# Attention and gated FFN on one core: the second to sixth pairs' queries reach the other row half by SBUF-to-SBUF transfers, with a new order of the work

## The chip, the cores and the metric

The kernel runs on one core of a Trainium2 chip. The metric is the device time of one execution in microseconds (us), the median of three runs. A profiled execution comes beside them, and all rows below are from it.

## What is computed

Queries, keys and values come as 4 batches of 8 heads, 1152 rows of 64 numbers, in float32. Neighbouring query rows are averaged, so 576 queries stand against 1152 keys. The attention's result goes through a feed-forward block with a gate.

```python
q_pool = q.reshape(B, H, S // 2, 2, D).mean(axis=3)
scores = (1 / np.sqrt(D)) * np.matmul(q_pool, k.transpose(0, 1, 3, 2))
attn = softmax(scores)                       # rowwise, with the maximum taken off
x = np.matmul(attn, v)                       # then heads side by side: (4, 576, 512)
h = np.maximum(x @ w_in, 0.0)                # (4, 576, 1024)
conv = sum(conv_w[t] * shifted(h, t) for t in range(3))
out = (h * sigmoid(conv)) @ w_out            # (4, 576, 512)
```

## The kernel before, in words

Two heads make a pair (16 pairs, four to a batch). The head with e = 0 has its queries in partitions 0 to 63 of a tile, the one with e = 1 in 64 to 127. `loads` brings in a pair: the keys to a `kt` tile, the values, and the queries to `qin`, of which there is a single buffer for all pairs. It then adds the two query rows that are to be averaged (`sum_q`, L305, on POOL or DVE), and makes two tiles from the sum: `qt` (`keep_q`, L308, ScalarE, all 128 partitions and 640 columns) and `qd` (`turn_q`, L313 on DVE or L318 on ScalarE, 64 partitions and 512 columns each, twice), which holds the same numbers with the two heads' row halves exchanged. A head's scores against half of its keys come from `qt`, and against the other half from `qd`, since those keys lie in the other row half of `kt`. So all of a pair's scores but those of its last 64 queries need both tiles.

`softmax` takes a pair through five steps of 128 queries (the fifth has 64). In each step and head: the scores (PE, L466), their maximum (DVE, L479), the exponential with its sum (ACT, L484), a small sum and its inverse (ACT L497 or DVE L501, then DVE L507). Most heads then write the normalised probabilities as two float16 parts (`hl`: the high one on ACT L532 or POOL L527, the low one on DVE L535) and have them turned by a DMA transpose (SP, L549). Eight heads (the set `X32`, one or two in each of the first four pairs, one in the fifth, the sixth and the tenth) normalise in float32 (L572 on POOL or DVE, L568 on ACT), are turned by PE (L586), and copied out of PSUM into `pt` by ACT (L595) or DVE (L597). `values` multiplies by the values (PE, L618 and L624) and splits the result (L640, L646, L651). `feed` and `second` are the feed-forward block (PE L713, L934, L940, L928). The weights' tidying up at the start runs through ACT L1017 and L1069, DVE L1030 to L1046, POOL L1021 and DVE or POOL L1050.

Nothing here is ordered by the compiler. All work is written down as tasks, and three tables set the rest: `ORDER` is the order in which the tasks are issued, each on the queue of its engine; `SLOTS` says which buffer of a ring a tile gets; `SWAPPED` names the tasks that run on their second engine (ACT instead of POOL, DVE instead of ACT, and so on). Each engine, and SP with its DMA issues, works through its own queue strictly in order. All loads, stores and transposes are issued by SP, on one DMA queue.

Of the kernel before, what the change touches and what calls it, by code (L numbers as in the profile page):

```python
# [94 lines left out]
cIcGaacMcOcNcPcHhtcJcKasabachucYhwadcQaecRhvafcThxcShPaghycUahhzhScXhAcWhBcVhQaic5cLathIaBhEhThRc4auhLhMavhFaw  # L95
hJhNhKaxibhUayazhOhVaAhWh4hCicajbEhGcZc8hDdriehHeoiddohXh5ifc7hsaCdah6c9aDaEh7aFhYh8aGhZh9akaHc0ixigiaalaIh0c1
ihamaJh2iiiyijiAh1aKbFh3andcimiziqikiBinaoiliodbirapiCdpiTc6isaqipiDivaLiEiUitiFiwjgiuaMiViMiKjhiGiLiHiIaNariR
aOiWjjiSaTc2iXaPjii3iJiPjkiNiYjyiOiQjlaQi6jzi4aRi7ddiZjBjmdsaUdwi0jnaVi5i1jCaSjvi8jAa2jwi2deaWjDaXdudtaYjQjoi9
jEdvdfjFaZjtjGdhdJjTa0dijxjudja3jRjpbGjrjqa4c3jUjsjJjNjSjcdka5a1dljOdmbbdnjVdMjKa6dOjWjLjddLjXa7j8j5jPjYjMbcjH
j9dgjZjIbdkbj0a8kabedqj3a9kcj1j4kqdNbfkddPkDj6d5bakedxbgj7kfkrknkgbhkskokLj2bwktdybiklkMkEkOkmd8kpkudzkNkjkPkh  # L100
bjkyk3kQbkkkkvkBk4bxkik6kRkCkSkwk0blkzkTbmkAkxbnk5dBdCk7fnkWewbybokYkXbsdDkUdEk1llk8dFk2lmdGealokVk9ebdHkHbqla
lplbdKlibpd9ljlqbHkZlkbrlnlclDbIkIlrldlsbJlAltlelEd7lgdIlGlhdQlBlFludRbKlVlHlfbLdSlwlvlWlIbubUlyd4epdTlxlXlCmg
btlJlzlKlYlLlSdVmhmjbVdWbWlOmklMlPlNlQdXlTl8mibzbXmlbAlZdYbBbYdZbZmmlUd0mnmvb0dAmyd2mol0mwlRl9mpb1mBmzmqmamtbM
mCmAmrl3mud1mQmDl1d6msl6mEl7l4mFmRl2mNmGmTl5mSjamxmLmUesmJmKbNmHjbmOm8mVbOmMm9nbmIkFedmPbPetmckGbQeud3bRmWbSmX
ncbTm5nabCdUm6b2mYnqndm7mbevm3mdbvm4m1nem2nDnfnrnnb3eJngerb4ecb5eenob6nsnhefb7nLb8nEnteLninjnMnFmZnknOm0menunv
nGbDb9ehDznyeinNcinPnpnlkJDAejnwn3nQDBnBeknmeln6eNDCemnRnCnSn4nTnWnzC7nAnxcjn7DUckC8n5clnUDlDVC9cmnZDmDan0nXn8
# [1142 lines left out]
```

## Time and profile before

| | |
|---|---|
| median of three runs | 605.52 us (605.26 to 607.05) |
| the profiled execution | 606.64 us |
| its span, first to last instruction | 604.8 us |
| mean granted clock of TensorE | 0.997 of 2.4 GHz |
| PE busy | 576.2 us (95%) |
| DVE busy | 563.0 us (93%) |
| ACT busy | 446.3 us (74%) |
| POOL busy | 282.6 us (47%) |
| DMA queue q1, share of 16 engines' span | 84.7% |

The profiled execution lasted 606.64 us; 1.84 us of it lie outside the span, and it is 1.12 us above the median. Busy time says how long an engine had at least one instruction running. An engine's shares are means over stretches of different kinds: before the first keys have landed nothing can run, then the weights and the first pairs share the engines, then attention and feed-forward alternate, and at the end only the feed-forward block is left.

### The profile page before, as it was taken

The numbers are of one execution on the slowest core, as the hardware profiler recorded it, in microseconds if no ns is written. First come the engines' busy times: TensorE is split into PE (matmuls) and PEld (weight loads), VectorE is DVE, ScalarE is ACT, GpSimd is POOL, SyncE is SP. The second block draws the span as 40 slices with busy tenths as digits, with TensorE's granted clock in tenths as the row PEclk, the third lists the DMA queues.
The fourth block names the chain that finished last, engine by engine and source line by source line (L and its number), as shares of the span: only waits on it lengthen the run. The fifth ranks groups of instructions, "written<-read, shape, count | busy, mean of one in ns | idle before, by whom it ended". The sixth has DMA issues, their size and how long they took to land.

```text
span 604.8 us, 11969 instructions
## 1 busy us (share of the span) xinstructions
PE 576.2 (95%) x4454; PEld 349.7 (58%) x4454; DVE 563.0 (93%) x911; ACT 446.3 (74%) x854; POOL 282.6 (47%) x300
## 2 busy tenths in 40 slices
PE   5989988799999999999999999999999999999997
PEld 2545555366665665556565665565657456775753
DVE  4999999899999999999999999999999999999881
ACT  4999999889999988767786956567567766776431
POOL 1563644626454533463545655645532435434530
PEclk9999999899999999999999999999999999999999
DMA  4944959684949899999999699899897999997601
GB/s 152 351 151 128 178 111 256 130 191 94 214 86 276 167 184 224 192 220 209 193 196 212 151 209 224 150 216 222 212 204 168 191 175 166 171 177 140 103 18 62
DMA packets 266713, 106.97 MB, mean 177 GB/s; under 512 B 254368, under 2 KB 255648, under 8 KB 266656
## 3 DMA queue, kind: packets, MB, share of 16 engines
q1 hardware_dynamic: 266656, 106.21, 84.7%
q8 instruction: 35, 0.57, 0.4%
q14 instruction: 22, 0.18, 0.1%
HBM read 37.77 MB, written 4.72 MB: 70 GB/s over the span
## 4 chain that ended last, share of the span: by engine, by line
PE 38%; DVE 15%; issue 4%; ACT 4%; POOL 3%; DMA 2%; SPq 0%; POOLq 0%; DVEq 0%; ACTq 0%
PE s L466 9%; PE a L934 8%; PE a L618 7%; PE a L713 7%; DVE hl L535 6%; DVE sm L479 4%; PE a L928 3%; DVE g L742 3%; POOL hl L527 2%; DMA pt<-hl 2%; PE a L940 2%; ACT p L484 1%; PE a L624 1%; DVE g L752 1%; PE a L586 1%
## 5 line engine op out<-in xcount | busy, mean ns | idle before, releaser
L484 ACT ACTIVATE p<-s,sm 128x1152 f32<-128x1152 f32 x144 | 175.3, 1218 | 57.2 <-DVE sm L479 24.2
L479 DVE TENSOR_REDUCE sm<-s 128x1 f32<-128x1152 f32 x144 | 193.1, 1346 | 10.8 <-PE s L466 10.4
L466 PE MATMUL s<-kt,qt 64*128 64x128 f32 (+2 forms) x704 | 183.1, 473 | 8.5 <-DMA kt<-in_k_dram 5.0
L535 DVE SCALAR_TENSOR_TENSOR hl<-p,sm,hl 128x1152 f16<-128x1152 f32 (+1 forms) x111 | 160.6, 1453 | 2.2 <-POOL hl L527 1.5
L527 POOL TENSOR_SCALAR hl<-p,sm 128x1152 f16<-128x1152 f32 (+1 forms) x65 | 85.7, 1322 | 129.0 <-DVE sm L507 82.0
L466 PE MATMUL s<-kt,qd 64*128 64x512 f32 x256 | 144.6, 647 | 1.0 <-DMA kt<-in_k_dram 1.0
L618 PE MATMUL a<-pt,v 128*64 128x256 f16 (+2 forms) x1512 | 111.9, 271 | 1.8 <-DMA pt<-hl 1.8
L466 PEld LDWEIGHTS s<-kt,qt 64*128 64x128 f32 (+1 forms) x704 | 77.3, 175 | 51.3 <-ACT p L484 20.9
L713 PE MATMUL a<-x,wi 128*128 128x257 f16 (+3 forms) x864 | 103.8, 274 | 1.5 <-ACT h L724 0.7
L713 PEld LDWEIGHTS <-wi 128*128 128x128 f16 x864 | 77.2, 98 | 37.5 <-issue 18.3
L618 PEld LDWEIGHTS <-v 128*64 128x64 f16 x1512 | 86.7, 110 | 20.3 <-issue 15.5
L735 POOL TENSOR_SCALAR g<-h,cw 128x255 f32<-128x255 f32 (+3 forms) x69 | 51.6, 751 | 61.5 <-ACT h L724 53.9
L934 PE MATMUL a<-wo,g 128*128 128x512 f32 x160 | 75.7, 606 | 0.5 <-ACT h L724 0.5
L742 DVE SCALAR_TENSOR_TENSOR g<-h,cw,g 128x255 f32<-128x255 f32 (+3 forms) x144 | 70.9, 512 | 4.3 <-POOL g L735 3.9
L586 PEld LDWEIGHTS a<-ident,p 128*128 128x128 f32 (+1 forms) x360 | 37.3, 142 | 56.3 <-ACT pt L595 16.2
L532 ACT ACTIVATE hl<-p,sm 128x1152 f16<-128x1152 f32 (+1 forms) x46 | 57.6, 1252 | 15.8 <-DVE sm L507 8.1
L572 POOL TENSOR_SCALAR p<-p,sm 128x1152 f32<-128x1152 f32 (+1 forms) x32 | 43.6, 1363 | 49.5 <-DVE sm L507 39.0
L586 PE MATMUL a<-ident,p 128*128 128x128 f32 (+1 forms) x360 | 55.4, 277 | 10.9 <-ACT pt L595 7.0
L624 PE MATMUL a<-pt,v 128*64 128x256 f32 (+1 forms) x288 | 64.1, 409 | 0.0
L724 ACT ACTIVATE h<-a,bs 128x257 f32<-128x257 f32 (+3 forms) x64 | 30.7, 482 | 28.1 <-PE a L713 16.6
L934 PEld LDWEIGHTS a<-wo,g 128*128 128x128 f32 x160 | 28.1, 190 | 37.3 <-issue 32.5
L595 ACT ACTIVATE pt<-a 128x384 f32<-128x384 f32 (+2 forms) x93 | 42.5, 474 | 6.4 <-PE a L586 6.2
(140 smaller groups left out, 655.6 us busy)
## 6 DMA issues: line engine op xcount, KB each, us to landing
qin<-in_q_dram SPq DMA_DIRECT2D x15, 640.0 KB, 4.7
kt<-in_k_dram SPq DMA_DIRECT2D x15, 576.0 KB, 5.5
vin<-in_v_dram SPq DMA_DIRECT2D x9, 576.0 KB, 4.9
g<-in_moe_w_in_dram SPq DMA_DIRECT2D x8, 512.0 KB, 5.3
w<-in_moe_w_out_dram SPq DMA_DIRECT2D x8, 512.0 KB, 4.7
out_dram<-o SPq DMA_DIRECT2D x16, 256.0 KB, 3.1
pt<-hl SPq DMA_TRANSPOSE x120, 5.0
v<-in_v_dram SPq DMA_DIRECT2D x6, 288.0 KB, 4.2
```

What stands on the lines that cost most here:

```text
L466: nc.tensor.matmul(out=w, lhsT=f, rhs=kk, start=True, stop=True)
L479: nc.vector.tensor_reduce(out=sm[:, e:e + 1], in_=runs(st[e]), axis=AX.XY, op=ALU.max, negate=True)
L484: nc.scalar.activation(out=p.tile().rearrange("p (a n) -> p a n", a=2), in_=runs(st[e]), func=AF.Exp, bias=sm[:, e:e + 1], scale=1.0, accu ...
L527: eng.tensor_scalar(out=hl[rows, 0], in0=ps_[e][rows], scalar1=sm[rows, 6 + e:7 + e], scalar2=1.0, op0=ALU.mult, op1=ALU.mult,)
L532: nc.scalar.activation(out=hl[rows, 0], in_=ps_[e][rows], func=AF.Copy, scale=sm[rows, 6 + e:7 + e])
L535: nc.vector.scalar_tensor_tensor(out=hl[rows, 1], in0=ps_[e][rows], scalar=sm[rows, 6 + e:7 + e], in1=hl[rows, 0], op0=ALU.mult, op1=ALU.s ...
L586: nc.tensor.transpose(w[:, (i - a1) * nq:(i - a1 + 1) * nq], ps_[e][rows, i * P:(i + 1) * P], ident[rows, rows])
L618: nc.tensor.matmul(out=to, lhsT=o.v[:, e, c, vc:vc + D], rhs=o.pt[y, e][:, hl * NC + c, 0:n], start=(c == 0 and j == 0), stop=(c == NC - 1 ...
L624: nc.tensor.matmul(out=to, lhsT=o.v[:, e, c].bitcast(F32), rhs=p32.rearrange("p (a n) -> p a n", a=NC)[:, c, 0:n], start=(c == 0), stop=(c ...
L713: nc.tensor.matmul(out=w[:, 0:n], lhsT=wi[:, a, j, f * P:(f + 1) * P], rhs=x.x[:, c, s0:s0 + n], start=(i == 0 and j == 0), stop=(i == 2 a ...
L742: nc.vector.scalar_tensor_tensor(out=c, in0=h[:, t:t + tok], scalar=cw[:, f, t:t + 1], in1=c, op0=ALU.mult, op1=ALU.add)
L934: nc.tensor.matmul(out=w.tile(), lhsT=g[f // 4][:, f % 4, c:c + P], rhs=wo[:, f, :], start=(f == 0), stop=(f == FC - 1),)
```

## The change

For the pairs 1 to 5 (the second to the sixth) `turn_q` is gone. Instead SP issues two transfers from `qt` to `qd`, one for each head, of 64 partitions by 512 float32 (128 KB), after `keep_q` has written `qt`. The pair's scores wait for `keep_q` and both transfers. Pair 0 and the pairs 6 to 15 do as before. The three tables are new as well: the order on every queue, the buffers, and which tasks run on their second engine.

```diff
             tq = add("ACT", act(n, 0.03), lambda cols=cols: keep_q(cols), after=[t], uses=[o.qin] + ([o.qt] if i else []),
                      takes=[] if i else [o.qt])
-            ready = [tq] + [
+            if 1 <= o.pr <= 5:
+                def swap_q(e):
+                    nc.sync.dma_start(out=o.qd.tile()[D - D * e:P - D * e, :], in_=o.qt.tile()[D * e:D * e + D, 0:K1])
+
+                ready = [tq] + [
+                    add("SP", 0.3, lambda e=e: swap_q(e), after=[tq], uses=[o.qt] + ([o.qd] if e else []),
+                        takes=[] if e else [o.qd], dma=0.9) for e in range(2)
+                ]
+            else:
+              ready = [tq] + [
                 add("ACT", act(turned.stop - turned.start, 0.16), lambda eng, e=e, turned=turned: turn_q(eng, e, turned), after=[t],
                     uses=[o.qin] + ([o.qd] if e or i else []), takes=[] if e or i else [o.qd],
                     alt=("DVE", 0.08 + (turned.stop - turned.start) / 1900.0, True)) for e in range(2)
...
 ORDER = """
-cIcGaacMcOcNcPcHhtcJcKasabachucYhwadcQaecRhvafcThxcShPaghycUahhzhScXhAcWhBcVhQaic5cLathIaBhEhThRc4auhLhMavhFaw
+eccIewcYcGaacMcJcOcNcPcHhtcKasabcLbEcQacc7adhuhwaehvcUafcRcThxcScVhPatcWaghyahhzaihShAhQhBcZaBcXhIhRc5hChTauhE
...
```

The counts of instructions that the order prints, before and now: on ACT `qd<-qin 64x512` 25 and 20, `qd<-qin 64x256` 1 and 0, `hl<-p,sm 128x1152` 41 and 39, `v<-vin,vs 128x18x64` 3 and 1, `v<-vin,vs 128x9x64` 2 and 4, `x<-xf,bs` 2 and 5. On DVE `qd<-qin 64x512` 5 and 0, `qd<-qin 64x256` 1 and 2, `p<-p,sm 128x1152` 2 and 1, `xf<-a,vs 128x320` 2 and 0. On POOL `hl<-p,sm 128x1152` 64 and 66. On PE the counts are the same. On SP `qd<-qt 64x512` 0 and 10.

Lines behind L327 stand nine lines further down in the changed kernel: L549 is L558 there, L595 is L604, L484 is L493, L1017 is L1026, L1069 is L1078 and L1013 is L1022.

The first place is SP's queue around the second pair (pair 1). Before, with the pair's queries loaded first and no transfer:

```order
8 L267 DMA qin<-in_q_dram 128x1280
9 L272 DMA v<-in_v_dram 128x1152
10 L1013 DMA g<-in_moe_w_in_dram 128x1024
11 L264 DMA kt<-in_k_dram 128x1152
12 L1013 DMA g<-in_moe_w_in_dram 128x1024
13 L1013 DMA w<-in_moe_w_out_dram 128x1024
14 L272 DMA v<-in_v_dram 128x576
15 L264 DMA kt<-in_k_dram 128x1152 x2
```

and now, with the two transfers (L329) and a load of weights between them:

```order
11 L1022 DMA g<-in_moe_w_in_dram 128x1024
12 L267 DMA qin<-in_q_dram 128x1280
13 L1022 DMA g<-in_moe_w_in_dram 128x1024
14 L264 DMA kt<-in_k_dram 128x1152
15 L272 DMA vin<-in_v_dram 128x576
16 L329 DMA qd<-qt 64x512
17 L1022 DMA g<-in_moe_w_in_dram 128x1024
18 L329 DMA qd<-qt 64x512
19 L264 DMA kt<-in_k_dram 128x1152 x2
```

The keys of later pairs (the row with x2) stand behind both transfers now, and the second transfer stands behind a load that has to wait for a free buffer of `g`.

The second place is ACT's queue at the same pair. Before, with the copy to `qd` (L318) ahead of the one to `qt` (L308):

```order
18 L595 ACTIVATE pt<-a 128x3x128
19 L1069 ACTIVATE g,ws<-wo 128x512
20 L351 ACTIVATE x,vs<-v 128x2x576
21 L484 ACTIVATE p,sm<-s,sm 128x1152
22 L1017 ACTIVATE g<-g 128x512
23 L318 ACTIVATE qd<-qin 64x512
24 L308 ACTIVATE qt<-qin 128x640
25 L595 ACTIVATE pt<-a 128x3x128 x2
```

and now:

```order
20 L1078 ACTIVATE g,ws<-wo 128x512
21 L1026 ACTIVATE g<-g 128x512
22 L604 ACTIVATE pt<-a 128x3x128 x3
23 L493 ACTIVATE p,sm<-s,sm 128x1152 x2
24 L604 ACTIVATE pt<-a 128x3x128
25 L308 ACTIVATE qt<-qin 128x640
26 L604 ACTIVATE pt<-a 128x3x128
27 L1078 ACTIVATE g,ws<-wo 128x512
```

The copy to `qd` is gone, and the copy to `qt` comes one exponential and four copies to `pt` later than it did.

## Rows read from the trace of the kernel before

**Rows 1.** Busy time by stretch; columns: window, length, PE, PEld, DVE, ACT, POOL, clock, DMA, GB/s.
```profile
0.00:15.12 15.12, 8.36 (x23) 3.97 (x24) 7.54 (x14) 7.16 (x15) 2.93 (x11) 1.00 0.48 152
15.12:136.08 120.96, 108.95 (x754) 62.20 (x751) 115.15 (x191) 109.91 (x215) 59.73 (x61) 0.99 0.75 187
136.08:211.68 75.60, 73.62 (x562) 47.84 (x561) 73.99 (x126) 70.28 (x131) 40.31 (x40) 1.00 0.76 167
211.68:408.24 196.56, 195.84 (x1450) 119.09 (x1447) 191.40 (x279) 141.82 (x258) 98.44 (x97) 1.00 1.02 199
408.24:559.44 151.20, 147.97 (x1251) 91.18 (x1248) 147.04 (x232) 102.96 (x195) 65.54 (x68) 1.00 0.97 183
```

**Rows 2.** Waits of the whole core, 15.12 to 136.08 us: total us, times, longest.
```profile
PEld a L586 <- ACT pt L595: 11.7, 17, 1.0
PE a L586 <- ACT pt L595: 7.0, 12, 1.7
PEld s L466 <- ACT p L484: 5.4, 8, 1.2
PE s L466 <- ACT p L484: 2.1, 5, 0.7
```

**Rows 3.** Groups by line and form, 15.12 to 136.08 us: count, busy us, mean ns.
```profile
L318 ACT ACTIVATE qd<-qin 64x512 f32<-64x512 f32 x6 | 3.8, 629 | 0.1
L313 DVE TENSOR_SCALAR qd<-qin 64x512 f32<-64x512 f32 x4 | 1.7, 422 | 0.1
```

**Rows 4.** Groups by line and form, whole span.
```profile
L532 ACT ACTIVATE hl<-p,sm 128x1152 f16<-128x1152 f32 x41 | 51.4, 1252 | 15.8 <-DVE sm L507 8.1 <-issue 2.3 <-DVE vs L369 1.3
L568 ACT ACTIVATE p<-p,sm 128x1152 f32<-128x1152 f32 x6 | 7.5, 1252 | 0.3 <-DVE sm L507 0.2
L405 ACT ACTIVATE v<-vin,vs 128x576 f16<-128x576 f32 x2 | 1.6, 780 | 0.0
L644 ACT ACTIVATE x<-xf,bs 128x256 f16<-128x256 f32 x2 | 1.0, 516 | 0.0
L731 ACT ACTIVATE g<-h,cw 128x255 f32<-128x255 f32 x2 | 1.0, 515 | 0.0
L484 ACT ACTIVATE p<-s,sm 128x1152 f32<-128x1152 f32 x144 | 175.3, 1218 | 57.2 <-DVE sm L479 24.2 <-DVE hl L535 17.6 <-POOL hl L527 3.2
L595 ACT ACTIVATE pt<-a 128x384 f32<-128x384 f32 x79 | 37.2, 487 | 5.8 <-PE a L586 5.6
```

**Rows 5.** Timelines of ACT, DVE, PE and SP at pair 1: start, length us.
```profile
25.15 0.75 ACT L308 ACTIVATE qt<-qin 128x640 f32<-128x640 f32 x1
33.01 0.42 DVE L313 TENSOR_SCALAR qd<-qin 64x512 f32<-64x512 f32 x1
35.62 0.37 PE L466 MATMUL s<-kt,qt 64*128 64x128 f32 x1
27.83 0.33 SPq L1013 DMA_DIRECT2D g<-in_moe_w_in_dram  x1
```

**Rows 6.** DMA issues: count, KB each, median us to landing.
```profile
g<-in_moe_w_in_dram SPq DMA_DIRECT2D x8, 512.0 KB, 5.3
out_dram<-o SPq DMA_DIRECT2D x8, 64.0 KB, 2.1
out_dram<-o SPq DMA_DIRECT2D x16, 256.0 KB, 3.1
qin<-in_q_dram SPq DMA_DIRECT2D x1, 384.0 KB, 6.1
```

**Rows 7.** Busy time in stretches around a gap of PE; columns as in rows 1.
```profile
107.50:109.00 1.50, 0.00 (x0) 0.00 (x0) 1.50 (x2) 1.45 (x3) 1.50 (x2) 1.00 1.35 280
109.00:112.00 3.00, 2.89 (x9) 1.23 (x9) 1.11 (x1) 2.27 (x4) 2.62 (x3) 0.57 0.41 142
112.00:113.20 1.20, 1.20 (x7) 1.02 (x6) 1.05 (x1) 0.22 (x1) 0.00 (x0) 0.64 0.00 0
```

**Rows 8.** Chain that ended last, in order of time: start, length us.
```profile
422.04 7.24 DMA pt<-hl
```

More of the change, by code (lines that the diff above doesn't have):

```diff
@@ new lines @@
+j5jYjpj9drkbjPjqdgj6bcjZkabdkcbGj0kqjda9kdj7bej3krj1j4kLbabfkeksbgkDbwbhdPj2ktkfkMknkgdxbikukodybjklkvkOkmbxkp
+kEbkkNkykhkPkjkiblkwkQk3kkbmkxkRdzkzkSk4k0kTkBk6kCdAk1k5kWbyk7kAd8kXkUdBllbnk8dCbsdDdEkYdFkVlmlok9bqdGkZladHd9
+kHlibolpdKk2lbljlnbplqeabrlgdRlDbHlhbIlrlGkIlsdSlEltlklclebJldlAlHlFlulBlfeplVlvd7bKlIbLlylWlwbUbzlJlKmgbteblX
+lClLlzmhmjlYlxbulSdTlMmklOlNlPdVdWlQbVlTl8mibWmlbAdXdYbBbXlZdZbYl0l3lUmmmyl9bCbZd2mBmnb0mvmomzd0b1mtd3lRmCmumr
+mpmsdUbMl1mql4mDl6mwl2mAmQd1mEl7d6mFmamGmxl5mTmRmNmSkFmHmUbDbNmLm8mOmMmJbOmImVmPm9esmcedbPeekGbQmWd4mXbRm5mbbS
@@ new lines @@
+mKm6nanbbTkJjanqncmdmYb2eternDeJndbvm7jeefnenfnrngnnjbegnonjb3nLnknEb4mekKnsnhb5m3b6nintb7nFfgmZnum4b8m0m1nGnv
+ehb9nMnOm2nyeicinNnlejekDzelnPeLnmemC7DAnwnQnBn3enC8nxnRDBn6cjnSn4nTnCeueNnzeqeMDlDCnpnWnAn5n7DUckDmC9nUnZDVn0
+nXDWnVn8cln1cmooDncnolnYDoexcon9nHcpoaomoeobeOopn2eZongvcaoceyDaodoqDXojDYoDDpDZDborokDDnIosohoEotnJofowoGDcog
+evoiouoFoxDse1oyoHovcbozDqoVDEDdccezoADtoIDreBDecdeCD0DuceoJDGDfoKDvoOoWDgoBDHoCDwoPoXcfoTnKpgcgoQDhpjoUcheDoY
+phoLoRDIcqDxoZo8pko0fzo3DioSDypieEoMDjDFploNjfo4mfpyo1e2pBo9pmo5eFpnpzpopro2o6DNo7ppcreYD1DOe3DPpCpqeGpsD2cspt
@@ new lines @@
+DJpupAD8ctDkcupvDQpDpweHpQcveKpEpxpTeIpFcwD9e4pRcxpcpGfhDRD3pUpSEapHpJDSD4pIpVDKD5pMD6pWEbqqDLpdpXpNp1eQpKqrcy
+pOpYp8pPpLqsDTfjp4p9p2p5p3p6DMqtquqbp7pZqveRqyEtqcp0qaeSqdqwqzqLqAD7qeqOczqfqMqgEuqBEfeTqjqCqPqNqhqoEgqZEheUqQ
+qiqpEvqmq0qkcAqneAq2qlcBq1qREwqSExqDqxqWq3EyqTqXEcq4qUrdflq5EirgqVEzq6eVrareeWEmqErhq7EHqYEnrfrbEOq8rirrEjq9rj
+EPrkcCfkrurlrsEkqHrorvrtrcEofmElrmrprwEprFrqrxEIryeXrCEVrzqIrGEJrWrHrDrnrOEdEQrXERrYfxrIcDe0rJESrErKrArZsaEqcE
+ErEWrPrLr0EAfAsbr1cFEXrNscEee5ePEsr2soEKrBEBE1r3ELfCfEsdr4spETfBEYr7e6serMECr5E9EZr8sqe7FaEDsfr9e8EEsre9fDfasg
@@ L154 @@
+    "11210013011100101001123120001032000103030021100001131102003000100011001101133011312112101200002020011210011130"
+    "0021311100201031010310120011001001"
 )
 SWAPPED = """
[L156 to L158 removed]
@@ L159 @@
[L159 to L161 removed]
+ahalaqauaDaIaMaVa4a9bdbibqbsbybGbObWb4ccckcscAcMcOcPcUcWcXc8dmdsdGd0emgShzhHhVh1isiuiDiLiOjejmjojujvjEjGjKjNke
+kmkvkFk9lblilrlAlSlYmmmEmImNmWnengnnnAnEnJnRnToboeogoroAoJoYpapepmpEpJpLpNpYqeqgqpqtqFqJqWq7rjrlrorxrzrQrUr4r7
@@ L162 @@
+slswsIsNsTsVs1s5tdtftrtttKtVtYucuguouquGuIu0u9vgvlvnvvvHvLvTvVvYv7v9wcwlwqwzwEwMwSwWw4w9xixnxwxBxKxMxPxXx3x7yf
+yhykytyvyyyHyMyVyXy0y6y8zezizmzuzzzIzNzWzYz1AaAcAfAlAtAxAAABAOAXAZA2BbBdBpBrBABIBMBQBYCcCeChCqCvCECPCRCXC1C5DB
+DIDPDWD3EaEhEoEvECEJEQFtFAFHFOFVF2F9GgGmGnGuGBGIGPGWG3HaHNHUH1H8IeIfImIsItIAIHIOIVI2I9JgJnJuJDJFJPKwKDKKKRKYK5
+LcLjLsLuLyLFLMLTL0L7MeMlMuMwMzMAMHMNMOMVM2M9NfNgNmNn
 """
```

101 lines of the change are left out of this document (39 added, 62 removed).

## The prediction
> **What bounds the kernel now.** I read the busy times by stretch first, since the means over the whole span hide where time is left. TensorE is idle for 604.8 - 576.2 = 28.6 us in all. By stretch that is 6.8 us up to 15.1 (the first loads), 12.0 us from 15.1 to 136.1, 2.0 us up to 211.7, 0.7 us up to 408.2, 3.2 us up to 559.4, and the 3.9 us that remain at the end [rows 1]. PE's own work does not change in count, so a gain has to come out of these waits. The pairs 1 to 5 are prepared within the stretch with the 12.0 us. There DVE is busy for 95% (115.2 of 121.0), ACT for 91% (109.9) and PE for 90% (109.0): three engines that hand each step of the softmax round, none of them with much room. Behind it, from 211.7 to 408.2, PE is busy for 99.6%, and what is won ahead of that stretch passes through it.
>
> Next the waits in that stretch. The largest ones of PE and of its weight loads are for ACT: for the copies of turned probabilities (L595) 7.0 us on PE, and for the exponential that frees a score buffer (L484) 2.1 us [rows 2]. The waits of weight loads overlap PE's work, so only the PE rows are lost time. PE is thus held up by ACT more than by DVE, though DVE is the fuller engine, and it feeds ACT with the maxima.
>
> **The change part by part.** *Removed.* In the stretch six copies on ACT at 629 ns and four on DVE at 422 ns belong to the pairs 1 to 5: 3.8 us of ACT and 1.7 us of DVE [rows 3].
>
> *Moved.* With the tables also other work changes engine. I compared the two orders up to the same point, the first step of pair 6: on DVE the rows ahead of the 55th maximum, on ACT those ahead of the 55th exponential. By then DVE has five copies less (one more belongs to pair 6 and went to ACT): 5 x 0.422 = 2.1 us; its other differences run from -1.1 to +0.7 us a kind and sum to -0.1. So DVE is relieved by 2.2 us. On ACT five copies less give 3.1 us, four high parts (L532, 1.252) less 5.0 us, and one normalisation (L568) less 1.3 us. Against that stand two value splits (L405, 0.780) more, 1.6 us, five of L644 (0.516) more, 2.6 us, two of L731 (0.515) more, 1.0 us, and small ones, 0.4 us. So ACT is relieved by 3.1 + 5.0 + 1.3 - 1.6 - 2.6 - 1.0 - 0.4 = 3.8 us [rows 3, 4]. POOL takes the high parts; it is busy for half of the stretch [rows 1], so this is free, unless a high part is late there: then the low part on DVE waits.
>
> *What the relief is worth.* The lower end is nothing, if each step still waits for the engine that was not relieved at that step. The upper end is both in a row, 2.2 + 3.8 = 6.0 us, half of PE's idle time there. I take the middle between DVE's and ACT's, 3.0 us: PE waits for ACT, but ACT's maxima come from DVE.
>
> *Added: ten issues and ten transfers of 128 KB.* An issue takes SP 0.33 us [rows 5], 3.3 us for all. No row of PE in this stretch names a DMA [rows 2], and the DMA share there is 0.75 [rows 1], so I cost issues and traffic at nothing. With that cover gone, 1.3 MB at the 187 GB/s of the stretch would be 7 us of queue time.
>
> *Added: a wait on SP.* The transfers wait for `keep_q`, and all later issues wait behind them: at pair 1 two loads of keys, one of values, and the queries of pair 2. Those keys and queries are needed a pair or more later, so this is nothing too. In return `qin` is free after one copy instead of three, so later queries load earlier. That is no gain either, as no row of PE waits for queries here [rows 2].
>
> *Added: a longer way to the scores.* `keep_q`, issue and landing now come one after the other. At the pairs 2 to 5 the order leaves many softmax steps in between. At pair 1 it is tight. Before, `keep_q` ended at 25.9 and the last copy at 33.4, and the scores began at 35.62 [rows 5]. In the new order ACT has, ahead of `keep_q`, one exponential more (1.2 us and 0.2 for its sum), four copies to `pt` more (4 x 0.487) and a small sum more (0.2), and two copies to `qd` less (0.6 and 0.4): 2.3 us later, 28.2 [rows 4]. Between the two transfers stands a load of weights, which has to wait for a buffer that ACT gives back after a copy to `pt` and a sum over weights, 1.3 us later: 29.5. The second transfer is then issued near 29.9. Nearest in size are stores of 64 and 256 KB, which land after 2.1 and 3.1 us: 32.0 to 33.0, ahead of the scores. If it only lands with the load ahead of it, 5.3 us after 29.5, it is 34.8 to 35; by the slowest rows, 6.1 and 7.24 us after the issue, it is 36.0 to 37.1, up to 1.5 us late [rows 6, 8]. I take 0.4 us, nearer to the stores and the load, with the ends 0 and 1.5.
>
> The Trainium skill (DMA: Bandwidth & Descriptors, section Anatomy of one DMA) states, for transfers issued by GpSimd, about 2.0 us for any transfer and its bytes at 436 GB/s on top. By it, as an estimate, 128 KB would land after 2.3 us, this term would be 0 and the time 602.5. No run here shows it for a transfer within SBUF.
>
> *At the start* the first sum went from POOL to DVE and the first two exchanged copies stand on DVE. The second half of the first keys is issued one load later in return. I cost both at nothing.
>
> **The sum.** -3.0 + 0.4 = -2.6 us. The profiled execution took 606.64 us, so one like it would take 604.0. It is 1.12 us above the median of 605.52, and against the median the forecast is 602.9 us. With both bounds of the relief and the wait it runs from 599.5 (all 6.0) to 607.0 (no relief, 1.5 of waiting). A measurement of this kernel can tell about 0.3% from no change, which is 1.8 us: faster means below 603.7, slower above 607.3.
>
> **The rivals.** *Forecast, 602.9, chance 0.50*, of which 0.43 lie below 603.7. For it speak that both engines that hold up PE are relieved in the stretch where PE waits, and that PE is the bound behind it.
>
> *DVE decides, 604.8, chance 0.20.* DVE is the fullest engine from 15 to 136 and busy for 97% up to 559 [rows 1]. If its order sets the pace there too, ACT's relief is worth nothing, and of DVE's 2.2 us about half comes through, since a maximum taken earlier then waits for its scores: 1.1 - 0.4 = 0.7, which gives 604.8. Against it speaks PE's 99.6% from 211 to 408.
>
> *The second transfer of pair 1 is late and the clock falls, 608.9, chance 0.17; this is the way to a slower kernel.* Before, PE stood still for the whole stretch from 107.5 to 109.0, and from 109.0 to 113.2 the granted clock was 0.57 and 0.64, most of the way to the lower level of 1.2 GHz. That cost 3.0 x 0.43 + 1.2 x 0.36 = 1.7 us beyond the standstill [rows 7]. If the transfer lands 1.7 us or more after PE has come to the scores, which is the length of the longest wait there [rows 2], the same happens again: 1.7 + 1.7 = 3.4 us. PE is then the late engine, ACT and DVE run into full buffers, and their relief is worth nothing: 605.5 + 3.4 = 608.9. It decides from a landing at 37.3, 7.4 us after the issue; the slowest landing in the rows is 7.24 us [rows 8]. The load of 512 KB right ahead of it speaks for it.
>
> The Trainium skill (DMA: Bandwidth & Descriptors, section Queues, rings and completion order) says that a queue's descriptors are taken in ring order on each DMA engine. By that the transfer would come behind the weights in any case, which is this rival's condition. The trace's single queue q1 agrees, but no row shows a small transfer behind a large one.
>
> *The new order decides elsewhere, 599.7, chance 0.13.* The tables are new to the end. In the stretch from 408 to 559 PE idles for 3.2 us [rows 1]. If these go as well, it is 602.9 - 3.2 = 599.7; if they double, 606.1. This is also the case in which the transfers don't do what they are put in for: gain or loss would then be in a stretch without any. I give 0.10 to the first and 0.03 to the second.
>
> **How the numbers follow.** Faster: 0.43 + 0.10 = 0.53. The same: 0.07 + 0.20 + 0.03 = 0.30. Slower: 0.17. The range from 599.5 to 609.0 takes in the bounds of both terms and the time of the slower rival; beyond its ends remain about 0.08 on each side. The forecast's own range is 599.5 to 604.5.
>
> **What would show it.** Right: PE's idle time from 15 to 136 us is about 9 us instead of 12.0, the waits for L595 (now L604) and L484 (now L493) are shorter, the first scores of pair 6 come some 3 us earlier, and PE is full from 210 to 400. The ten transfers land in 2 to 5 us, and PE waits for none but perhaps the second one of pair 1. Wrong: a row in which PE waits for `qd<-qt` for over 1.5 us with a lower granted clock behind it; DVE without a gap and PE with as much idle time as before; or an unchanged first 210 us and a difference after 400.

## The result, and the profile after

The changed kernel took **609.41 us** (median of 4 runs, 608.85 to 610.29) beside 605.75 us for the kernel before (4 runs, 605.26 to 607.05). The ratio is 1.0064, with an interval from 1.0044 to 1.0084: slower by 3.9 us, where 2.6 us less was forecast. The profiled execution took 609.48 us with a span of 607.7; against the 604.8 of before, that is 2.9 us more.

The first view is the busy time by stretch of the changed kernel, in the columns and stretches of [rows 1].

```profile
0.00:15.12 15.12, 7.50 (x20) 3.31 (x22) 7.44 (x14) 7.07 (x15) 1.28 (x10) 1.00 0.71 245
15.12:136.08 120.96, 109.10 (x757) 64.52 (x757) 114.72 (x190) 105.40 (x210) 69.52 (x61) 0.97 0.75 185
136.08:211.68 75.60, 73.26 (x570) 48.42 (x569) 74.36 (x122) 70.17 (x135) 39.13 (x37) 1.00 0.74 169
211.68:408.24 196.56, 192.38 (x1401) 114.79 (x1396) 190.50 (x280) 142.08 (x250) 97.45 (x93) 1.00 1.00 194
408.24:559.44 151.20, 149.55 (x1217) 92.94 (x1218) 146.86 (x226) 102.13 (x197) 70.06 (x69) 1.00 0.98 190
```

Against [rows 1], TensorE's idle time from 15 to 136 us is 11.9 us and was 12.0: nothing of the 3 us that were to go from there. From 212 to 408 us, where PE was busy for 99.6%, it idles for 4.2 us and not 0.7. From 408 to 559 us it idles for 1.7 us and not 3.2. The last but one column, the DMA share, is the time of all packets over that of 16 DMA engines; more is said of it below.

The second view is the waits of PE from 15.12 to 136.08 us, which answer to [rows 2].

```profile
PEld s L475 <- ACT p L493: 10.0, 14, 1.8
PEld a L595 <- ACT pt L604: 9.1, 16, 1.2
PE s L475 <- ACT p L493: 4.4, 7, 1.0
PE a L595 <- ACT pt L604: 3.7, 8, 0.9
PE a L595 <- POOL p L581: 1.1, 1, 1.1
```

The waits for the copies of turned probabilities fell from 7.0 to 3.7 us, as the change was to do. Those for the exponential rose from 2.1 to 4.4 us, and the one for GpSimd's normalisation is 1.1 us, where two such waits were 0.9 us together. ScalarE itself waits longer for VectorE's maxima in this stretch; the first line is from the kernel before, the second from the changed one.

```profile
ACT p L484 <- DVE sm L479: 0.6, 3, 0.3
ACT p L493 <- DVE sm L488: 3.8, 7, 1.5
```

ScalarE's busy time fell by 109.91 - 105.40 = 4.5 us, and 3.2 us of that stand here as waiting for VectorE. Over the whole span these waits grew from 24.2 [rows 4] to 47.7 us, most of it behind 212 us, where no copy was taken away.

The third view is the issue of the ten transfers on SP's queue (duration in ns min/median/max, first and last start) and their time from issue to landing in the changed kernel.

```profile
L329 SPq DMA_DIRECT2D qd<-qt x10: 467/525/1393, 28.9 to 160.3; - x10
DMA to landing us min/median/max: 2.3/4.4/4.8
```

They land after 2.3 to 4.8 us, and nothing waited for them: PE's waits name none of them. At pair 1 the second transfer was issued at 30.2 us and landed at 34.9, and the scores began at 35.6 us, as before.

### The profile page after: what moved, and what is told of

Same layout as the page of the kernel before. It is cut to its first block, busy times and chain, and to the rows that moved or that the text cites. A ratio compares the mean times of both kernels' runs of the same rounds, so it can differ in the third digit from the quotient of the medians.

```text
span 607.7 us, 11962 instructions
## 1 busy us (share of the span) xinstructions
PE 575.1 (95%) x4454; PEld 351.6 (58%) x4454; DVE 563.1 (93%) x906; ACT 443.2 (73%) x851; POOL 295.3 (49%) x298
## 4 chain that ended last, share of the span: by engine, by line
PE 52%; DVE 21%; ACT 6%; issue 4%; POOL 2%; DMA 1%; SPq 0%; ACTq 0%; POOLq 0%; DVEq 0%
PE s L475 15%; PE a L722 9%; PE a L943 9%; PE a L627 8%; DVE sm L488 6%; DVE hl L544 5%; DVE g L751 4%; PE a L633 4%; PE a L937 3%; ACT p L493 2%; PE a L949 2%; PE a L595 2%; ACT hl L541 1%; POOL hl L536 1%; DVE g L761 1%
## 5 line engine op out<-in xcount | busy, mean ns | idle before, releaser
L493 ACT ACTIVATE p<-s,sm 128x1152 f32<-128x1152 f32 x144 | 175.3, 1219 | 65.0 <-DVE sm L488 47.7
L536 POOL TENSOR_SCALAR hl<-p,sm 128x1152 f16<-128x1152 f32 (+1 forms) x67 | 92.7, 1387 | 102.1 <-DVE sm L516 63.4
L627 PEld LDWEIGHTS <-v 128*64 128x64 f16 x1512 | 87.9, 110 | 19.2 <-issue 15.1
L751 DVE SCALAR_TENSOR_TENSOR g<-h,cw,g 128x255 f32<-128x255 f32 (+3 forms) x144 | 73.4, 531 | 2.8 <-POOL g L744 2.4
L581 POOL TENSOR_SCALAR p<-p,sm 128x1152 f32<-128x1152 f32 (+1 forms) x33 | 46.4, 1406 | 53.0 <-DVE sm L516 48.5
L595 PEld LDWEIGHTS a<-ident,p 128*128 128x128 f32 (+1 forms) x360 | 36.9, 141 | 49.9 <-ACT pt L604 14.4
L541 ACT ACTIVATE hl<-p,sm 128x1152 f16<-128x1152 f32 (+1 forms) x44 | 55.1, 1252 | 14.3 <-DVE sm L516 6.3
L595 PE MATMUL a<-ident,p 128*128 128x128 f32 (+1 forms) x360 | 54.4, 276 | 8.4 <-ACT pt L604 4.5
L604 ACT ACTIVATE pt<-a 128x384 f32<-128x384 f32 (+2 forms) x94 | 42.9, 473 | 5.6 <-PE a L595 5.2
L475 PEld LDWEIGHTS s<-kt,qd 64*128 64x128 f32 x256 | 42.0, 192 | 2.4 <-issue 1.7
```

The costliest lines, as they stand in the source:

```text
L475: nc.tensor.matmul(out=w, lhsT=f, rhs=kk, start=True, stop=True)
L493: nc.scalar.activation(out=p.tile().rearrange("p (a n) -> p a n", a=2), in_=runs(st[e]), func=AF.Exp, bias=sm[:, e:e + 1], scale=1.0, accu ...
L536: eng.tensor_scalar(out=hl[rows, 0], in0=ps_[e][rows], scalar1=sm[rows, 6 + e:7 + e], scalar2=1.0, op0=ALU.mult, op1=ALU.mult,)
L541: nc.scalar.activation(out=hl[rows, 0], in_=ps_[e][rows], func=AF.Copy, scale=sm[rows, 6 + e:7 + e])
L595: nc.tensor.transpose(w[:, (i - a1) * nq:(i - a1 + 1) * nq], ps_[e][rows, i * P:(i + 1) * P], ident[rows, rows])
L627: nc.tensor.matmul(out=to, lhsT=o.v[:, e, c, vc:vc + D], rhs=o.pt[y, e][:, hl * NC + c, 0:n], start=(c == 0 and j == 0), stop=(c == NC - 1 ...
```

## The experiments

All kernels ran beside the kernel before. Its median was 605.4 to 606.9 us in the five groups of runs, so ratios are compared, and a difference of ratios is turned into time with 605.5 us. An interval of a ratio is about 0.2% to either side, 1.2 us.

### Transfers, copies and the new order apart

Four kernels take the change apart: the old tables with transfers, both tables with neither copies nor transfers, and the new tables with copies.

```diff
 before_transfers: the changed kernel's code, with the tables of the kernel before
-ready = [tq] + [turn_q, turn_q]
+ready = [tq] + [swap_q, swap_q]
 before_none, after_none
-f = (o.qt if half == e else o.qd)[r, d * P:(d + 1) * P]
+f = (o.qt if half == e or 1 <= o.pr <= 5 else o.qd)[r, d * P:(d + 1) * P]
 (and turn_q, or swap_q, returns at once for these pairs)
 after_copies: the code of the kernel before, with the changed kernel's tables
-ready = [tq] + [swap_q, swap_q]
+ready = [tq] + [turn_q, turn_q]
```

> The tables of the kernel before, with the ten transfers in place of the ten copies of the pairs 1 to 5; keep_q of a pair stands where the first of its three steps stood, the transfers where the other two stood. If the relief of ACT and DVE is worth what the prediction said (3.0 us) and the transfers hide, 602 to 604 us. If DVE sets the pace in the first 200 us (ACT's relief worth nothing), 604.5 to 606. If the transfers themselves make the kernel slower (late landing, or SP held up), 608 to 610, as in the changed kernel.

> The kernel before without the ten copies and without transfers: the pairs 1 to 5 take both halves of their scores from qt, so half of their scores are made with the other head's queries. This is the relief alone. If relief is worth 3.0 us, 602.5 to 603; if DVE decides, 604 to 605.5, since only 1.7 us of DVE's work go; if transfers cost something, this is faster than the tables of before with transfers, else the same within 1 us.

> The changed kernel with its transfers left out: the pairs 1 to 5 take both halves of their scores from qt, as in the kernel before without copies. If the transfers cost time, 605 to 607 us. If the new order costs it and the transfers are free, 609 to 610 as with them.

> The tables of the changed kernel with copies on ACT (six) and DVE (four) in place of the transfers, each where the transfer stood or, where the next pair's queries are loaded earlier, just ahead of that load. If the transfers are worth 3.0 us in this order, 612 to 613; if relief is worth nothing, 609 to 610; if the transfers are what makes the changed kernel slow, 606 to 607.

| kernel | median, us | ratio to before | interval |
|---|---|---|---|
| before_transfers | 604.87 | 0.9983 | 0.9964 to 1.0003 |
| before_none | 604.98 | 0.9975 | 0.9952 to 0.9998 |
| the changed kernel | 609.41 | 1.0064 | 1.0044 to 1.0084 |
| after_none | 609.57 | 1.0067 | 1.0044 to 1.0089 |
| after_copies | 612.94 | 1.0104 | 1.0080 to 1.0129 |

Three things follow. **The transfers cost nothing that can be told**: with and without them the ratios are 0.9983 and 0.9975 in the old order, 1.0064 and 1.0067 in the new. **Taking the copies off ScalarE and VectorE is worth 1.0 us in the old order** (1.0000 to 0.9983), which its interval does not tell from nothing, and 2.4 us in the new one (1.0104 to 1.0064). Both runs on the old tables came out where VectorE was expected to set the pace. In the profiles the 1.0 us is not made where the copies were: the 55th maximum, at pair 6, starts at 201.85 us in the kernel before and at 201.84 with transfers. **The new tables cost 4.9 us** (0.9983 to 1.0064); that is the whole loss and more.

### Where the new order loses: four spliced orders

Four orders take one kernel's tables up to a point and the other's behind it, with the transfers throughout.

```diff
 after_head
-ORDER, SLOTS, SWAPPED of one kernel
+the first 1180 tasks as in the changed kernel, the rest as in the kernel before
 after_tail
+the first 1195 tasks as in the kernel before, the rest as in the changed kernel
 after_last_part
+the first 1540 tasks as in the kernel before, the rest as in the changed kernel
 before_start
+the first 300 tasks as in the kernel before, the rest as in the changed kernel
```

> The changed kernel's order, buffers and second engines up to the beginning of the ninth pair (its first 73 exponentials, about 270 us), and the order of the kernel before from there on, with the ten transfers throughout; one clearing of an x buffer is moved. The kernel before with transfers alone took 604.87 us, the changed kernel 609.41. If the new order loses its time behind 270 us (where its trace has new waits of TensorE at 289, 301 and 398 us): 604 to 605.5. If it loses it ahead of that (a later first maximum, a longer stretch of half clock after 113 us): 608.5 to 610. If both halves lose some: 606 to 608.

> The reverse: the order of the kernel before with the ten transfers up to the ninth pair (its first 74 exponentials, about 270 us), and the changed kernel's order from there on; one clearing of an x buffer is moved. If the loss is behind 270 us: 608.5 to 610. If it is ahead of it: 604 to 605.5. If both lose some: 606 to 608, and with the run of the reversed halves the two losses add up to 4.5 us.

> The order of the kernel before with the ten transfers up to its 96th exponential (about 353 us), the changed kernel's order from there on. The changed kernel's maxima fall from 2.2 us ahead at the 75th to 3 us behind at the 87th, between 281 and 325 us, and stay there. If the loss is made in that stretch, this kernel is at 604 to 606 while the one cut at 270 us is slow. If the wait at 398 us and the end make it, this one is at 608 to 610 as well.

> The order of the kernel before with the ten transfers for the first 17 exponentials (about 64 us), the changed kernel's order from there on. The changed kernel's first maximum comes 1.6 us later. If the start carries through to the end: 607.5 to 608. If what is late at the start is made up by the middle (the difference at the 55th maximum was 0): 609 to 610. If the start also causes the longer stretch of half clock at 113 us: 606 to 607.

They took 614.86, 617.30, 609.50 and 614.15 us, with ratios of 1.0148, 1.0197, 1.0068 and 1.0142. All four are slower than the old order and three are slower than both, which no theory had expected. The busy times around the splice near 270 us show why; the first two rows are after_head, the third after_tail, in the columns of [rows 1].

```profile
257.00:281.00 24.00, 21.88 (x138) 11.81 (x136) 20.61 (x30) 13.48 (x23) 10.60 (x12) 1.00 1.09 226
281.00:305.00 24.00, 19.63 (x135) 11.55 (x136) 18.69 (x27) 15.23 (x28) 6.33 (x8) 0.86 0.76 165
```

```profile
281.00:305.00 24.00, 18.72 (x126) 11.03 (x126) 17.46 (x24) 13.39 (x26) 9.99 (x11) 0.79 0.77 163
```

TensorE idles for 2.1 and 4.4 us, and for 5.3 us, right behind the splice, and the granted clock falls to 0.86 and 0.79 there. The other two show the same behind theirs: 5.9 us from 64 to 88 us in before_start (the old order with transfers has 2.0 there) and 2.4 us from 354 to 378 us in after_last_part (none), each at a clock of 0.86. The seam costs as much as what was looked for, so these runs say nothing on the place of the loss. Nor do the maxima show one place, as was taken for after_last_part: the 75th starts at 276.2 us in the old order with transfers and at 276.1 in the changed kernel, the 87th at 318.8 and 320.3, the 101st at 374.7 and 374.8, the 121st at 455.1 and 459.6. They do say that two good orders joined are not a good one.

### Mending the new waits

The changed kernel's timeline of PE has three waits of about 1 us behind 212 us that the old order with transfers does not have. Two of them, with the idle time ahead and what ended it:

```profile
302.08 0.32 PE L372 MATMUL a<-ident,vs 128*128 128x128 f32 x1 [1.34 <-ACT h L733]
399.62 0.37 PE L475 MATMUL s<-kt,qt 64*128 64x128 f32 x1 [1.33 <-ACT p L493]
```

The third is one of 0.88 us at 483.77, for L733 again. Each has a step on the releasing engine that could go first. The start was mended in the same way.

```diff
 mend_middle, ScalarE at 299 us
+L733 h<-a
 L541 hl<-p
 L860 kt<-wo
-L733 h<-a
 VectorE at 395 us
+L488 sm<-s
 L544 hl<-p
...
-L488 sm<-s
 ScalarE at 482 us
+L733 h<-a
 L493 p<-s
-L733 h<-a
 mend_start, VectorE at 8 us
+L488 sm<-s
 L1030 g<-g
 L1039 wo<-g
-L488 sm<-s
 ScalarE at 10 us
+L308 qt<-qin, L318 qd<-qin x2
 L493 p<-s
-L308 qt<-qin, L318 qd<-qin x2
 mend_both: all of it
```

> The changed kernel with three steps put earlier on their queues, nothing else: on ScalarE one copy out of PSUM (L733) ahead of a high part and a sum (at 299 us) and one ahead of an exponential (at 481 us), and on VectorE one maximum, with its scores, ahead of a low part (at 395 us). They are the releasers of the waits of TensorE of 1.34, 0.88 and 1.33 us that the changed kernel has at 300.7, 482.9 and 398.3 us and the kernel before with transfers does not. If these new waits are what the new order costs: 3.5 us less than the changed kernel's 609.4, 605.5 to 607. If each only gives way to the next wait behind it: 608.5 to 610. If the loss is elsewhere, in the clock or the start: 608.5 to 610 as well, with those three waits gone.

> The changed kernel with the first maximum ahead of two steps of the weights on VectorE, and on ScalarE the next queries' copy and the two exchanged ones ahead of the first exponential. If the late start (first maximum at 9.0 us and not 7.5, TensorE idle for 1.25 us at 10.7) carries through: 1 to 1.6 us less, 607.8 to 608.5. If the pairs behind it take up what is won: 609 to 610. If the half clock at 113 us comes from the pace that the start set: a further 1 to 1.5 us less.

> Both edits. If the new waits and the start together are the new order's cost of 4.6 us: 604 to 606, as the kernel before with transfers. If the gains do not add up: that of the better of the two. If neither counts: 609.

The ratios are 1.0078 (1.0058 to 1.0099), 1.0046 (1.0026 to 1.0065) and 1.0071 (1.0051 to 1.0090), with medians of 611.75, 609.65 and 611.37 us. Against the changed kernel's 1.0064 the start gave 1.1 us, within the intervals. The three waits of the middle gave nothing. PE's timeline of mend_both shows what came in their place:

```profile
301.85 0.37 PE L475 MATMUL s<-kt,qt 64*128 64x128 f32 x1 [0.65 <-ACT p L493]
370.51 0.37 PE L475 MATMUL s<-kt,qt 64*128 64x128 f32 x1 [0.78 <-ACT p L493]
399.34 0.37 PE L475 MATMUL s<-kt,qt 64*128 64x128 f32 x1 [1.40 <-ACT p L493]
407.75 0.37 PE L475 MATMUL s<-kt,qt 64*128 64x128 f32 x1 [0.85 <-ACT p L493]
```

The waits at 302 and 484 us are gone or shorter, the one at 399 us is there as before, and two new ones stand at 371 and 408 us. These three waits, taken one by one, are therefore not the cost of the new order: the idle time came back at other places. What it is that PE runs into there these runs do not show.

### Taking work off one engine in the full stretch

If TensorE is the bound from 212 us on, as the prediction had it, less work for it must shorten the kernel. The second batch's feed-forward, from 276 to 392 us, is done without part of its products, or without one tap on VectorE.

```diff
 less_dve_before, less_dve_after
 def tap(t, f=f, h=h, g=g):
+    if b == 1 and t == 2:
+        return
 less_pe_before, less_pe_after
-for i, (a, c) in enumerate(((0, 0), (0, 1), (1, 0))):
+for i, (a, c) in enumerate(((0, 0), (0, 1), (1, 0))[:2 if b == 1 else 3]):
```

> The changed kernel without the last of the three taps on VectorE (L751) in the second batch's feed-forward, which runs from 276 to 392 us: 16 steps of 0.48 and 0.54 us, 8.2 us of VectorE. If TensorE alone is the bound there (its order and its work): 609.4 less at most 0.5. If VectorE holds up the new order there: TensorE's 4.2 us of idle time from 212 to 408 us go, 605 to 606. If both engines are at their limit, something between: 607 to 608.5.

> The same 16 steps left out of the kernel before with transfers (604.87 us), where TensorE's idle time from 212 to 408 us is only 0.7. If VectorE doesn't hold that order up: 604 to 605. If its steps set the pace of both orders: as much less as in the changed kernel, 4 us or more.

> The changed kernel without the third of the three products (L722) in the second batch's feed-forward, from 276 to 392 us: 64 matrix products, a third of 8 groups of 1.48 and 8 of about 1.75 us, 8.6 us of TensorE. If TensorE alone is the bound there: 600.8 to 602. If VectorE is: 608 to 609.5, the time becomes waits of TensorE. If both: 604 to 607.

> The same 64 products left out of the kernel before with transfers (604.87 us). If TensorE alone is the bound there, as the prediction took it: 596 to 597.5. If VectorE, busy for 97%, is as near to its limit: 601 to 604.

| kernel | median, us | ratio to before | interval |
|---|---|---|---|
| less_pe_before | 607.57 | 1.0020 | 0.9994 to 1.0045 |
| less_dve_before | 603.95 | 0.9963 | 0.9945 to 0.9981 |
| less_pe_after | 609.75 | 1.0058 | 1.0037 to 1.0079 |
| less_dve_after | 610.77 | 1.0084 | 1.0058 to 1.0109 |

Some 8 us of work less, and none of the four is faster than its own order (0.9983 and 1.0064) beyond the intervals; less_pe_before is slower by 2.2 us, at the edge of what can be told. The busy times from 276 to 392 us, for the changed kernel, less_pe_after and less_dve_after in turn, columns as in [rows 1]:

```profile
276.00:392.00 116.00, 113.16 (x843) 69.89 (x843) 113.03 (x167) 86.73 (x158) 62.52 (x57) 1.00 1.00 196
```

```profile
276.00:392.00 116.00, 106.51 (x792) 63.68 (x791) 113.70 (x168) 87.36 (x158) 59.90 (x58) 1.00 1.01 197
```

```profile
276.00:392.00 116.00, 112.07 (x827) 68.97 (x827) 105.84 (x151) 85.72 (x157) 60.58 (x57) 1.00 0.98 196
```

The work left out turned into idle time of the engine that did it, and the other engine stayed where it was. In less_pe_after VectorE is busy for 98%, PE for 92%. In less_dve_after PE is busy for 97%, as in the changed kernel (98%), and DVE for 91%. In the old order it is the same: DVE 114.43 of 116 us in less_pe_before, PE 115.62 in less_dve_before. So each run leaves a second engine at its limit, and no run took work off both. The chain of work that ended last, followed back from the last instruction over the whole span, changes engine with it (its shares by engine, for the changed kernel, less_pe_after and less_dve_after):

```profile
PE 52%; DVE 21%; ACT 6%; issue 4%; POOL 2%; DMA 1%; SPq 0%; ACTq 0%; POOLq 0%; DVEq 0%
PE 35%; DVE 33%; ACT 6%; issue 5%; DMA 5%; POOL 2%; ACTq 0%; DVEq 0%; POOLq 0%
PE 54%; DVE 18%; ACT 7%; issue 4%; DMA 4%; POOL 1%; ACTq 0%; POOLq 0%; DVEq 0%; SPq 0%
```

The last column but one, the DMA share, is also as high as ever in all three: 1.00, 1.01 and 0.98.

One side result: less_pe_after had a granted clock of 1.00 from 15 to 136 us, where the changed kernel had 0.97, and the same time. Among the executions of after_none, too, one with a granted clock of 1.000 over the whole span took 610.65 us and the profiled one, with 0.994, 609.57. The clock that the changed kernel lost there is not the cause either.

```profile
15.12:136.08 120.96, 106.92 (x758) 62.84 (x759) 116.11 (x190) 105.69 (x212) 70.07 (x61) 1.00 0.76 184
```

### The DMA queue

From 212 to 559 us the DMA share is 1.02 and 0.97 in [rows 1], and 0.97 to 1.01 over the whole of it in every run on the two uncut orders. This share is no measure of what the engines can carry at most: it is 1.09 over 24 us of after_head, shown above, and 1.35 over 1.5 us in [rows 7]. Most of it are the transposes of probabilities (`pt<-hl`), 120 in all. Their issue rows (duration on SP's queue in ns min/median/max, first and last start) are, for the kernel before, for the old order with transfers, and for the changed kernel:

```profile
L549 SPq DMA_TRANSPOSE pt<-hl x120: 1252/2744/7407, 51.9 to 563.6; - x120
```

```profile
L558 SPq DMA_TRANSPOSE pt<-hl x120: 1274/2772/7157, 53.7 to 561.8; - x120
```

```profile
L558 SPq DMA_TRANSPOSE pt<-hl x120: 1275/2798/6888, 50.1 to 568.3; - x120
```

Span less start of the last transpose is 604.8 - 563.6 = 41.2, 603.0 - 561.8 = 41.2 and 607.7 - 568.3 = 39.4 us. It is 41.1 to 41.2 in before_none and both runs of the old order with work left out, and 39.3 to 39.4 in after_none, after_copies, the three mended orders, early_keys and both runs of the new order with work left out. So each order has a fixed end behind its last transpose, 1.8 us shorter in the new one, and the new order's last transpose comes 6.5 us later than that of the old order with transfers. 6.5 - 1.8 = 4.7 us, the whole difference of the two spans. But the end is as fixed behind the last low part, which VectorE makes for a transpose, and so it does not tell the queue from what feeds it (old order with transfers, then the changed kernel; 603.0 - 558.8 = 44.2 and 607.7 - 563.3 = 44.4 us):

```profile
L544 DVE SCALAR_TENSOR_TENSOR hl<-p,sm,hl x111: 1398/1412/2314, 48.5 to 558.8; 128x1152 f16<-128x1152 f32 x105, 64x1152 f16<-64x1152 f32 x6
L544 DVE SCALAR_TENSOR_TENSOR hl<-p,sm,hl x111: 1392/1411/1958, 48.0 to 563.3; 128x1152 f16<-128x1152 f32 x105, 64x1152 f16<-64x1152 f32 x6
```

How many transposes had been issued by a given time was to tell where they fell behind. By 212 us it is 25 in both orders. By 276 us (DMA issues from 0 to 276: count, KB each, median us to landing), in the old order with transfers and in the changed kernel:

```profile
kt<-in_k_dram SPq DMA_DIRECT2D x9, 576.0 KB, 5.8
pt<-hl SPq DMA_TRANSPOSE x44, 5.0
```

```profile
kt<-in_k_dram SPq DMA_DIRECT2D x8, 576.0 KB, 5.3
pt<-hl SPq DMA_TRANSPOSE x43, 5.5
```

One transpose and one load of keys less in the changed kernel. By 400 us the two are level again, with 75 transposes and 12 such loads each, and by 550 us it is 116 and 114. Leaving 8 us of TensorE's or VectorE's work out changes the counts at 550 us by at most one: 116 and 115 in the old order, 114 and 114 in the new. With 95 of the 120 transposes behind 212 us, one comes every (561.8 - 212) / 95 = 3.68 us in the old order and every (568.3 - 212) / 95 = 3.75 us in the new. That says no more than that the kernels take as long as they take.

The queue's idle time ahead of that was the candidate for the loss. These rows are the busy times from 196 to 220 us of the old order with transfers, then of the changed kernel.

```profile
196.00:208.00 12.00, 11.83 (x78) 7.11 (x77) 11.87 (x17) 11.71 (x23) 8.16 (x8) 1.00 0.77 151
208.00:220.00 12.00, 12.00 (x98) 7.99 (x95) 11.97 (x20) 10.55 (x19) 3.22 (x3) 1.00 0.94 179
```

```profile
196.00:208.00 12.00, 11.62 (x78) 6.78 (x76) 11.97 (x18) 10.79 (x24) 7.55 (x8) 1.00 0.45 106
208.00:220.00 12.00, 12.00 (x99) 7.92 (x97) 12.00 (x20) 9.43 (x15) 3.79 (x3) 1.00 0.80 148
```

(0.77 - 0.45) x 12 + (0.94 - 0.80) x 12 = 5.5 us of the DMA engines stand empty in the new order that the old one uses. The engines beside it look alike; nothing in PE's or DVE's columns betrays it. But the window was chosen where the two differ. Over all of the first 212 us the two orders move almost the same (old order with transfers, then the changed kernel; the last column is GB/s):

```profile
0.00:212.00 212.00, 191.09 (x1337) 114.87 (x1339) 195.55 (x325) 184.40 (x354) 102.96 (x110) 1.00 0.76 184
0.00:212.00 212.00, 190.18 (x1344) 116.41 (x1345) 196.84 (x325) 182.74 (x358) 109.94 (x108) 0.98 0.74 183
```

Two runs add DMA work behind 276 us, and one brings a load forward.

```diff
 keys_twice_before, keys_twice_after
+for _ in range(2 if o.pr in (9, 11, 12, 13) else 1):
     nc.sync.dma_start(out=o.kt.tile()[:, cols], in_=k[o.pr][:, cols])
 early_keys, SP's queue
 L558 pt<-hl x2
+L264 kt<-in_k_dram
 L558 pt<-hl
...
-L264 kt<-in_k_dram
 L558 pt<-hl x4
```

> The kernel before with transfers (604.87 us), with the keys of the tenth, twelfth, thirteenth and fourteenth pair loaded twice, 4 x 576 KB more between 280 and 425 us. At the 408 GB/s that loads alone reach at a DMA share of 1.02 (20 to 26 us) that is 5.8 us of the queue. If the DMA queue sets the pace from 212 to 559 us: 609.5 to 611. If it has room to spare there: 604.5 to 606.

> The same four loads doubled in the changed kernel (609.4 us). If the DMA queue sets the pace: 614 to 615.5. If it has room, since TensorE waits elsewhere: 609 to 611.

> The changed kernel with one load moved on the queue: the keys of the tenth pair, whose buffer is free from about 200 us, ahead of the transpose of the sixth pair's last step (about 209 us) instead of near 290 us. The DMA share from 196 to 220 us is 0.45 and 0.80 there, where the kernel before with transfers has 0.77 and 0.94. If the DMA queue sets the pace from 212 us on, the load's 1.45 us (576 KB at 408 GB/s) leave the full stretch: 607.5 to 608.5. If it is not the queue's idle time ahead of the full stretch that the new order loses: 609 to 610.

The doubled loads took 616.33 us (ratio 1.0179, 1.0154 to 1.0204) and 624.37 us (1.0310, 1.0278 to 1.0341): 11.9 and 14.9 us more than without them, over twice the 5.8 us of their bytes. The waits of SP's queue in keys_twice_before and then in keys_twice_after (270 to 440 us) say why:

```profile
SPq L265 <- DMA kt<-in_k_dram: 14.9, 4, 4.8
```

```profile
SPq L265 <- DMA kt<-in_k_dram: 12.1, 3, 4.9
```

The second load of a pair waited on the queue until the first had landed, and every transpose behind it waited too. The edit thus did more than it was to do, and is no clean measure of the bytes. It does show that when this queue stands still for some 4 us at a time, most of it goes to the end of the kernel: 11.9 us for 14.9 us of standing, and 14.9 for 12.1 with the bytes on top. That it has little slack against such standing is not yet that it sets the pace.

early_keys took 609.29 us (ratio 1.0059, 1.0038 to 1.0081), no difference from the changed kernel. That is where it was expected if the queue's idle time is not what the new order loses, though the 1.45 us at stake are hardly more than the interval. The DMA share from 208 to 220 us rose from 0.80 to 0.98, but that from 196 to 208 us stayed (busy times as above, then the issue row of its transposes):

```profile
196.00:208.00 12.00, 11.99 (x84) 7.05 (x86) 11.97 (x22) 10.96 (x20) 6.85 (x8) 1.00 0.46 89
208.00:220.00 12.00, 12.00 (x97) 8.30 (x94) 12.00 (x18) 9.22 (x16) 4.01 (x4) 1.00 0.98 184
```

```profile
L558 SPq DMA_TRANSPOSE pt<-hl x120: 1275/2800/6856, 49.7 to 567.2; - x120
```

The load was issued at 207.4 us, behind the larger hole instead of in it. Its last transpose starts 1.1 us earlier in the profiled execution, which the median does not confirm. A load that fills the hole at 196 us was not run.

**What is settled and what is open.** Settled: the new order is the loss; the transfers and the clock are not; taking 8 us off TensorE alone, or off VectorE alone, shortens neither order. Open: what sets the pace from 212 us on, and why it is slower in the new order. Two readings are left. The first is that TensorE and VectorE are both at their limit, so that either holds the kernel when the other is relieved. For it speak that the engine left alone stays busy for 97 to nearly 100% in each of the four runs with work left out, and that the chain changes engine; a run with work taken off both is missing. The second is the DMA queue. For it speak the doubled loads, and that from 212 to 559 us the high parts wait for a transpose to free their buffer for 9.0 us on GpSimd and 5.5 on ScalarE, where the old order with transfers has 4.9 and 0.4. Against it speak early_keys, the level counts at 400 us, the equal traffic up to 212 us, and that TensorE waits for transposes 0.5 us in that stretch of the old order with transfers and not at all in the changed kernel. No run took work off the queue there. Neither reading is shown.

No version with the whole computation beat the kernel before by more than can be measured. The old order with transfers, 0.9983 (0.9964 to 1.0003), is the best of them.

## Why the prediction was wrong

**The new order, left at nothing: the step that failed.** The sum has no term for the new tables but what they move between engines ahead of the 55th maximum. Only the fourth case spoke of the rest, and its loss was 606.1 us with a chance of 0.03, worked out from PE's idle time from 408 to 559 us. The tables measured +4.9 us, and with the edit alone at -1.0 us they make up the 3.9 us. That case's sentence "gain or loss would then be in a stretch without any" transfers is what happened, and so is "an unchanged first 210 us", named as a sign of being wrong; the difference shows ahead of 400 us already, as idle time of PE from 289 us on.

**The relief, -3.0 us.** Three times too large: 1.0 us in the order that it was worked out against, between the ends 0 and 6.0 but not told from 0 by its interval. In the new order the copies are worth 2.4 us, which is near the forecast, but that order needs them because it is worse. The count of work was near: up to the 55th maximum, at 201.8 us in both kernels, ACT is busy for 174.71 us where it was 178.56, 3.9 us less against 3.8 predicted. (Of the splits of `x` the traces have four more on ACT up to that point, not five.) DVE is busy for 186.66 us and was for 186.89, 0.2 us less and not 2.2, though it has the five copies less: part of what is left to it lasts longer, two sums of queries 1.19 us each and not 0.86. And ScalarE's relief became waiting for maxima, as the waits in the first section show. The step from less work to less waiting of PE is therefore what did not hold: PE's idle time from 15 to 136 us is 11.9 us and was 12.0, and at the 55th maximum the changed kernel is where the kernel before was, 201.80 and 201.85 us. This is the mechanism of the rival in which DVE decides, and its price, 0.7 us net, was nearer to what the relief alone gave.

**What bounds the kernel.** "Behind it, from 211.7 to 408.2, PE is busy for 99.6%, and what is won ahead of that stretch passes through it." Nothing was won ahead of it that could have passed. As a statement of the bound it is not enough: 8.6 us of PE's work less in that stretch did not shorten the kernel (less_pe_before, less_pe_after), so PE was not the bound there, or not alone. The same rows held the other candidates: VectorE with 97%, and a DMA share of 1.02 and 0.97 [rows 1]. Which of them holds the kernel beside PE stays open.

**Issues and traffic, 0.** Right, in both orders, to 0.1% of the ratio, though an issue took 0.47 to 1.39 us and not 0.33.

**The wait at pair 1, +0.4 us.** It did not come, and the steps to it were right: `keep_q` ended at 28.8 us (28.2 predicted), the second transfer was issued at 30.2 (29.9), and it landed at 34.9, which is the case in which it lands with the load ahead of it (34.8 to 35), ahead of the scores at 35.6. The transfers land after 2.3 to 4.8 us, inside the bounds of 2.1 to 7.24 that the rows gave. The Trainium skill (DMA: Bandwidth & Descriptors, section Anatomy of one DMA) gives a formula for transfers issued by GpSimd, by which 128 KB take 2.3 us, as an estimate; of these ten, issued by SyncE, the fastest took that, and the median 4.4.

**The start, 0.** Roughly right: PE idles 0.9 us longer up to 15.1 us, and mend_start gave 1.1 us, within the intervals.

**The rival on the slower side, 608.9 us,** came within about 0.5 us of the time and is wrong all the same. It asked for a late transfer, PE's wait for it and a lower clock behind. No wait names a transfer, and after_none, which has none, takes as long. The clock did fall again, to 0.50 from 113 to 118 us, but less_pe_after ran without that and was no faster. That the time came near is luck.

## What to carry to other kernels

A share of 99% says that an engine was occupied, not that it is the bound: look along the same row for every resource that is as full before letting a gain pass through a stretch, and take work off two engines at once where each alone changes nothing. A change that brings a new order is two changes; give the order a term of its own, and measure the edit in the old order first. When a wait is mended and a similar one appears further on, stop mending, and count the progress of a shared queue in both orders, at several times (here transposes issued by 212, 276, 400 and 550 us): a lag at one of them can be gone at the next.

## What was not expected of the hardware

The issue of a transpose lasts 2.77 us on SP's queue (median; 1.27 to 7.2), where that of a load of keys lasts 0.53 us. Over 120 transposes that is some 120 x 2.77 = 332 us of the queue that issues everything; how much of a long row is waiting the rows do not tell. The row for the loads of keys, old order with transfers:

```profile
L264 SPq DMA_DIRECT2D kt<-in_k_dram x17: 413/531/1281, 1.5 to 453.4; - x17
```

And 8 us of work can be taken off TensorE, or off VectorE, in a stretch where they are busy for 97 to 99%, and the kernel is no faster.
